# Scores on 64 instead of 32 partition rows, with the attention work moved to other places in the matmul stream, for batches 4 to 7

## The chip, the cores and the metric

One core of one Trainium2 chip. The metric is the device time of one execution in microseconds (us), as the median of several runs. The time before is 330.08 us. Runs of one kernel differ: those of the kernel before by up to 1.7% within the rounds of one chip (328.38 to 334.06). So every kernel is compared with runs of the kernel before on the same chip in the same rounds. Some runs are slow (more than 1.5% above the fastest of the same kernel). They take no part in any ratio, but are counted in the medians; of the profiles, only that of e3 is of a slow run.

## The reference

Two parts follow each other. The attention has 8 batches, 8 heads, 576 positions and 64 elements a head, and each head is computed twice: with a mask that leaves 7 neighbours, and on queries, keys and values that are averaged over 4 positions. The sum of both, as 4608 tokens of 512 features, goes through a feed-forward layer of 2048 features.

```python
def _attn_ref(q, k, v):                       # q, k, v: (8, 8, 576, 64) f32
    q_d = q.reshape(B, H, Sd, factor, D).mean(axis=3)      # factor 4; k_d, v_d too
    out_up = np.repeat(sm_attn(q_d, k_d, v_d), factor, axis=2)
    mask = np.abs(pos[:, None] - pos[None, :]) < factor
    scores = np.where(mask, scale * q @ k^T, -1e9)
    return out_up + softmax(scores) @ v
    # ... cut, written shorter
def _moe_ref(x, w_in, w_out):                 # (4608, 512), (512, 2048), (2048, 512)
    h = x @ w_in
    g = h * (1.0 / (1.0 + np.exp(-1.702 * h)))
    return (g @ w_out).astype(np.float32)
```

The inputs q and k are drawn with a factor of 0.1, which makes the softmax almost flat. So the check says little about the scores.

## The kernel before

The feed-forward layer runs in nine groups of 512 tokens. A group has 64 matmuls of the first product (16 slices of 4) and then 64 of the second, all 128x128 by 512 columns. Into this stream TensorE also gets the attention of the next batch, in seven pieces at fixed positions: position 0 to 15 is a slice of the first product, 16 and up counts the matmuls of the second.

```python
POS = [13, 16, 33, 42, 53, 62, 71]    # scores 0, exps 0, scores 1, values 0+1, values 2+3, transposes 0+1, 2+3

    for g in range(n_groups):
        b = g + 1
        # ... cut: group 0 has its own order
        elif b < B:
            if b > 2:
                load_v4(b)                       # SP: 6 DMAs, values to be averaged
            prep_qk(b, 0)                        # DVE: transposes k and q of heads 0 to 3 ("set 0")
            pool_qk(b, 0)                        # POOL: averages them
            if b + 1 < B:
                for qd in range(NQ):
                    load_qk(b + 1, qd)           # POOL: asks for the next batch's q and k
            prep_v(b, nc.gpsimd)                 # POOL: casts values to bf16
            if b + 1 < B:
                load_v(b + 1)                    # SP: 10 DMAs, next batch's values
            prep_qk(b, 1)                        # the same for heads 4 to 7 ("set 1")
            pool_qk(b, 1)
            prep_v4(b, nc.gpsimd)                # POOL: averages values
        # ... cut: the pieces of attention are put at POS; mm1, mm2
```

The DVE transposes take pairs of elements as one (the bitcast below). The kernel then reads a head of 64 elements from 32 partition rows, even and odd elements beside each other, and a score takes two matmuls of 32 rows (index `a`; 32*64 in the trace):

```python
    def prep_1(name, b, qd):
        # ... cut
        nc.vector.transpose(
            out=t32.rearrange("p (i c) -> p c i", c=18),
            in_=store[b, qd].bitcast(FP32).rearrange("p (c d) -> p c d", c=18),
        )

    def scores(b, qd, barred=False):             # 80 matmuls; scores_d: 24 in the same way
        # ... cut
        for i in range(5):
            for a in range(2):
                for par in range(2):
                    for r in range(4):
                        rows = slice(32 * r, 32 * r + 32)
                        # ... cut
                            lhsT=kT[b, qd][rows, k0 : k0 + 64, a],
                            rhs=qT[b, qd][rows, q0 : q0 + 60, a],
                            start=(a == 0 and not barred),
                            tile_position=(32 * r, 64 * par),
```

SP issues the value loads and the stores of the results, in program order. POOL issues the loads of q and k between its own sums.

The softmax here doesn't subtract the row's maximum and nothing guards it: scores larger than these inputs give would overflow.

## Time and profile before

330.08 us (329.90 to 331.29, 4 runs). The page of the kernel before, its span, engines, and two rows of its 40 slices (granted TensorE clock and DMA share in tenths):

```profile
span 329.5 us, 11220 instructions
PE 308.0 (93%) x4987; PEld 157.9 (48%) x5043; DVE 130.2 (40%) x215; ACT 184.1 (56%) x322; POOL 138.9 (42%) x168
PEclk9997999999999999999999999999999999999999
DMA  7999979999814991398339922993180110011011
```

TensorE (PE) is the bound (93% busy), at full clock (mean 0.995). The DMA row is not busy all the time: full for half a group, then nearly empty, and so on through groups 1 to 5.

Windows of the kernel before over groups 1, 3, 4 and 5. Columns: window and length, busy us (and instructions) of PE, PEld, DVE, ACT and POOL, then clock, DMA share and GB/s.

```profile
67.08:102.18 35.10, 33.30 (x594) 17.04 (x600) 17.43 (x27) 21.73 (x39) 17.52 (x19) 1.00 0.74 161
...
135.89:169.42 33.53, 32.63 (x594) 16.88 (x600) 16.33 (x25) 20.95 (x36) 17.53 (x19) 1.00 0.68 143
169.42:202.82 33.40, 32.50 (x595) 16.74 (x601) 16.34 (x25) 20.95 (x36) 17.51 (x19) 1.00 0.68 144
202.82:237.13 34.31, 32.79 (x594) 16.85 (x600) 16.33 (x25) 20.95 (x36) 17.51 (x19) 1.00 0.69 140
```

The 128 large matmuls of a group take 27.6 us (group 7, without attention). The rest of 33.4 us is attention, on the critical path because PE is nearly always busy.

PE's timeline of the kernel before at one score block (start, duration, what ran):

```profile
113.50 0.84 PE L351 MATMUL pa<-qT,kT 32*64 32x60 bf16 x80
114.14 0.59 PE L370 MATMUL pa<-qdT,kdT 32*64 32x144 bf16 x24
114.66 2.76 PE L618 MATMUL pm<-xT,w_in_bf 128*128 128x512 bf16 x11
```

From start to start, a block takes 114.66 - 113.50 = 1.16 us. That is what the change wants to halve.

SP's timeline of the kernel before in group 4 (start, us on its queue, what it issued):

```profile
170.67 2.95 SPq L226 DMA_DIRECT2D v<-in_v_dram  x6
179.43 8.90 SPq L214 DMA_DIRECT2D vf<-in_v_dram  x10
189.14 14.83 SPq L664 DMA_DIRECT2D out_dram<-osb  x4
```

An entry counts the waits inside it. The 14.83 us for four stores are almost all waiting for results; 0.33 us is one store. The value requests of 2.95 and 8.90 us are mostly issue time: over the whole run, one that loads values for the cast holds SP for a median of 0.64 us. In this kernel nothing that PE needs soon stands behind them.

### The profile page before, as it was taken

How to read it: one execution, taken by the hardware profiler on the slowest of the kernel's cores; microseconds unless marked ns; L12 is line 12 of the kernel's file. 1: busy time of each engine (PE TensorE's matmuls, PEld its weight loads, DVE VectorE, ACT ScalarE, POOL GpSimd, SP SyncE). 2: the span in 40 equal slices, each digit the busy share in tenths (PEclk: the TensorE clock that was granted, in tenths of full speed). 3: DMA queues.
4: the chain of work that ended last, by engine and by line, in shares of the span. 5: the costliest groups of instructions: out<-in, count | busy, mean ns of one | idle time of the engine just before them, and what ended most of it. 6: DMA issues, size and time to landing. Idle time of an engine off the chain costs nothing.

```text
span 329.5 us, 11220 instructions
## 1 busy us (share of the span) xinstructions
PE 308.0 (93%) x4987; PEld 157.9 (48%) x5043; DVE 130.2 (40%) x215; ACT 184.1 (56%) x322; POOL 138.9 (42%) x168
## 2 busy tenths in 40 slices
PE   8767999789999999999999999998999999999995
PEld 3444455445554455455544555455444544444444
DVE  4870512770468036802771277225730560000000
ACT  2552773375936683667367746674566646415611
POOL 7890844049603970298029901990098000000000
PEclk9997999999999999999999999999999999999999
DMA  7999979999814991398339922993180110011011
GB/s 126 184 188 208 171 151 183 196 210 236 191 39 132 205 207 39 116 193 171 102 100 200 200 83 86 196 195 105 40 172 2 60 41 32 2 72 56 2 62 65
DMA packets 63552, 41.36 MB, mean 126 GB/s; under 512 B 44048, under 2 KB 54416, under 8 KB 63504
## 3 DMA queue, kind: packets, MB, share of 16 engines
q1 hardware_dynamic: 55056, 26.95, 35.8%
q0 software_dynamic: 8304, 13.63, 23.9%
q8 instruction: 39, 0.64, 0.9%
q14 instruction: 9, 0.07, 0.1%
q10 hardware_dynamic: 144, 0.07, 0.1%
HBM read 44.83 MB, written 9.44 MB: 165 GB/s over the span
## 4 chain that ended last, share of the span: by engine, by line
PE 87%; issue 4%; SPq 3%; ACT 2%; DVE 2%; DMA 1%; DVEq 0%; ACTq 0%
PE pm L618 35%; PE pm L674 33%; PE pa L351 3%; SPq L214 3%; PE pa L618 2%; PE pa L431 2%; PE pa L409 2%; PE pa L370 2%; PE pa L458 2%; PE pa L674 2%; DMA vf<-in_v_dram 1%; PE pm L689 1%; PE pa L484 1%; ACT vd L321 0%; PE pa L312 0%
## 5 line engine op out<-in xcount | busy, mean ns | idle before, releaser
L618 PE MATMUL pm<-xT,w_in_bf 128*128 128x512 bf16 x528 | 120.3, 380 | 1.4 <-DVE xT L561 0.7
L674 PE MATMUL pm<-w_out_bf,gT 128*128 128x512 bf16 x493 | 114.1, 379 | 5.4 <-issue 5.2
L629 ACT ACTIVATE gT<-pm 128x512 bf16<-128x512 f32 x136 | 81.0, 598 | 45.2 <-PE pm L618 45.2
L618 PEld LDWEIGHTS <-w_in_bf 128*128 128x128 bf16 x576 | 55.8, 98 | 68.4 <-issue 2.5
L674 PEld LDWEIGHTS <-gT 128*128 128x128 bf16 x560 | 51.7, 98 | 59.5 <-issue 0.2
L276 POOL TENSOR_TENSOR pq<-kT 128x576 f32<-128x576 bf16 x16 | 18.5, 1157 | 105.0 <-DVE kT L260 96.1
L395 DVE TENSOR_TENSOR es<-es,mask 128x600 bf16<-128x600 bf16 x28 | 20.6, 749 | 92.0 <-ACT es L381 91.2
L659 ACT ACTIVATE osb<-pm 128x512 f32<-128x512 f32 (+2 forms) x35 | 20.7, 592 | 40.2 <-PE pm L674 36.1
L534 ACT COPY od<-pa 128x384 f32<-128x384 f32 (+1 forms) x56 | 18.4, 412 | 32.4 <-DVE y L444 18.7
L444 DVE TENSOR_TENSOR y<-pa,rc 128x896 bf16<-128x896 f32 x32 | 34.9, 1092 | 1.1
L555 DVE TENSOR_TENSOR xT<-pa,od 128x570 bf16<-128x570 f32 x28 | 21.1, 753 | 12.0 <-ACT od L534 11.9
L381 ACT ACTIVATE es<-pa 128x600 bf16<-128x600 f32 x32 | 19.8, 668 | 7.0 <-PE pa L351 6.8
L297 POOL TENSOR_TENSOR v<-v 112x512 f32<-112x512 f32 x18 | 22.8, 1265 | 0.0
L661 DVE TENSOR_SCALAR osb<-pm 128x128 f32<-128x128 f32 x1 | 0.3, 292 | 55.3 <-ACT osb L659 55.3
L260 DVE STREAM_TRANSPOSE kT<-kb 128x576 f32<-128x576 f32 x16 | 20.0, 1249 | 2.0 <-DMA kb<-in_k_dram 2.0
L260 DVE STREAM_TRANSPOSE qT<-qb 128x576 f32<-128x576 f32 x16 | 19.8, 1239 | 0.9 <-DMA qb<-in_q_dram 0.7
L276 POOL TENSOR_TENSOR pq<-qT 128x576 f32<-128x576 bf16 x16 | 18.4, 1148 | 0.0
L291 POOL CAST vb<-vf 128x2560 bf16<-128x2560 f32 (+1 forms) x11 | 17.6, 1618 | 0.0
L442 DVE RECIPROCAL rc<-pa 128x14 f32<-128x14 f32 x32 | 7.7, 240 | 21.7 <-PE pa L431 21.7
L351 PE MATMUL pa<-qT,kT 32*64 32x60 bf16 x1280 | 14.0, 203 | 1.5 <-issue 1.5
L351 PEld LDWEIGHTS <-kT 32*64 32x64 bf16 x1280 | 11.8, 104 | 6.7 <-issue 5.5
L300 POOL TENSOR_TENSOR vd<-v 112x256 bf16<-112x256 f32 x18 | 13.7, 759 | 1.4
(90 smaller groups left out, 247.0 us busy)
## 6 DMA issues: line engine op xcount, KB each, us to landing
vf<-in_v_dram SPq DMA_DIRECT2D x80, 128.0 KB, 4.7
out_dram<-osb SPq DMA_DIRECT2D x35, 256.0 KB, 2.1
v<-in_v_dram SPq DMA_DIRECT2D x36, 192.0 KB, 6.1
kb<-in_k_dram POOLq DMA_DIRECT2D x16, 288.0 KB, 6.8
qb<-in_q_dram POOLq DMA_DIRECT2D x16, 288.0 KB, 7.1
w_out_bf<-in_moe_w_out_dram POOLq DMA_DIRECT2D x4, 512.0 KB, 12.1
w_in_bf<-in_moe_w_in_dram POOLq DMA_DIRECT2D x2, 512.0 KB, 5.7
w_in_bf<-in_moe_w_in_dram POOLq DMA_DIRECT2D x1, 1024.0 KB, 10.7
```

What stands on the lines that cost most here:

```text
L260: nc.vector.transpose(out=t32.rearrange("p (i c) -> p c i", c=18), in_=store[b, qd].bitcast(FP32).rearrange("p (c d) -> p c d", c=18),)
L276: nc.gpsimd.tensor_tensor(out=t1, in0=sv[:, :, 0:2, :], in1=sv[:, :, 2:4, :], op=ALU.add)
L297: eng.tensor_tensor(out=t1[0:112], in0=x[:, :, 0:2, :], in1=x[:, :, 2:4, :], op=ALU.add)
L351: nc.tensor.matmul(sp[r // 2][64 * par : 64 * par + 64, r % 2, 60 * i : 60 * i + 60], lhsT=kT[b, qd][rows, k0 : k0 + 64, a], rhs=qT[b, qd] ...
L381: nc.scalar.activation(out=es[2 * qd + u][:, :, 0:300], in_=sp[u][:, :, 0:300], func=AF.Exp, scale=inv_sqrt_d,)
L395: nc.vector.tensor_tensor(out=ev, in0=ev, in1=mask, op=ALU.mult)
L444: nc.vector.tensor_tensor(out=y, in0=ov[:, :, :, 0:D], in1=rc.to_broadcast([128, 2, 7, D]), op=ALU.mult,)
L555: eng.tensor_tensor(out=sub(xT[hp], t0 + 3, (57, 2), (114, 5), (1, 57)), in0=sub(x, 3, (509, 2), (57, 5), (1, 57)), in1=sub(od, 3, (57, 2) ...
L618: nc.tensor.matmul(acc, lhsT=w_in_bf[:, dmc, ffc * 128 : (ffc + 1) * 128], rhs=xT[dmc][:, g * TG : g * TG + TG], start=(dmc == 0), stop=(d ...
L629: nc.scalar.activation(out=gT[:, ffc, :], in_=acc, func=AF.Silu, scale=GELU_SCALE)
L659: eng.activation(out=osb, in_=ap, func=AF.Copy, scale=1.0 / GELU_SCALE)
L674: nc.tensor.matmul(ops[t], lhsT=gT[:, ffc, t * 128 : (t + 1) * 128], rhs=w_out_bf[:, ffc, :], start=(ffc == 0), stop=(ffc == n_ffc - 1),)
```

## The change

The intent is to put a whole head of 64 elements on 64 rows, so that a score block needs 40 + 12 matmuls instead of 80 + 24. A second transpose of the same data and four SBUF-to-SBUF copies of 32 rows for each tile (k or q of one set) bring the odd elements beside the even ones. SP issues them, 64 in all. To give this chain time, the scores of batches 4 to 7 move one group earlier (a "rotated" pipeline), and loads, casts and sums are ordered anew. The diff, cut to its core:

```diff
+    ROWS64 = 4
 def prep_1(name, b, qd):
-        tt = work.tile([128, S, 2], BF16, ...)
-        nc.vector.transpose(...)
+        n = 2 if b >= ROWS64 else 1
+        tt = work.tile([128, 2, S, 2], BF16, ...)
+        for x in range(n):
+            # ... cut: the transpose, into tt[:, x]
+        if n == 2:
+            for x in range(2):
+                f = tt[:, x].rearrange("p t a -> p (t a)")
+                for r in range(2):
+                    src = 64 * r + 32 * x
+                    to = 64 * r + 32 * (1 - x)
+                    nc.sync.dma_start(
+                        out=f[to : to + 32, 0 : 2 * S - 1], in_=f[src : src + 32, 1 : 2 * S]
+                    )
 def scores(b, qd, barred=False):
+        if b >= ROWS64:                    # 40 matmuls, no accumulation
+            # ... cut: loops over j, i, par, u
+                            rows = slice(64 * u, 64 * u + 64)
+                                lhsT=kT[b, qd][rows, j, k0 : k0 + 64, 0],
+                                rhs=qT[b, qd][rows, j, q0 : q0 + 60, 0],
+                                start=True, stop=True,
+                                tile_position=(64 * u, 64 * par),
 # ... cut: scores_d and pool_qk in the same way; groups 0 and 2
-    POS = [13, 16, 33, 42, 53, 62, 71]
+    at(1, 0, load_qks, 3)                  # group 1, position 0, loads of q and k of batch 3
+    at(1, 0, prep_v, 2, nc.gpsimd)
+    at(1, 0, load_v, 3)
+    at(1, 0, prep_qk, 2, 1)
+    at(1, 0, load_qks, 4)                  # new in group 1
+    # ... cut
+    at(2, 68, s_all, 4, 0, False, True)    # scores of batch 4, set 0
+    at(3, 0, prep_v, 5, nc.gpsimd)
+    at(3, 0, prep_qk, 4, 1)                # copies of batch 4, set 1
+    # ... cut
+    at(3, 15, s_pe, 4, 1)
+    at(3, 52, s_all, 5, 0, False, False)
+    at(3, 64, s_all, 5, 1, False, True)
+    for g in range(4, B - 1):
+        b, c = g + 1, g + 2
+        if c < B:
+            at(g, 0, prep_v, c, nc.gpsimd)
+            at(g, 0, prep_qk, c, 0)        # copies of set 0
+            at(g, 0, pool_qk, c, 0)
+            at(g, 0, load_v4, c)
+            if c + 1 < B:
+                at(g, 0, load_v, c + 1)    # values, between the two sets of copies
+            at(g, 8, prep_qk, c, 1)        # copies of set 1
+            at(g, 8, pool_qk, c, 1)
+            if c + 1 < B:
+                at(g, 8, load_qks, c + 1)
+            at(g, 8, prep_v4, c, nc.gpsimd)
+            at(g, 42, s_all, c, 0, True, False)
+            at(g, 60, s_all, c, 1, False, True)
+        at(g, 6, avn, b, P01)              # values and transposes, now early
+        at(g, 11, avn, b, P23)
+        at(g, 16, tr, b, P01)
+        at(g, 25, tr, b, P23)
```

More of the change, by code (lines that the diff above doesn't have):

```diff
@@ L66 @@
     kdT = [persist.tile([128, 160, 2], BF16, name=f"kdT{i}") for i in range(NQ)]
+    kdP = [persist.tile([128, 2, 160], BF16, name=f"kdP{i}") for i in range(NQ)]
     PA = [psum.tile([128, 2, 512], FP32, name=f"pa{i}") for i in range(3)]
@@ L124, in fill @@
             nc.vector.memset(t[:, SD:160, :], 0.0)
+        for t in kdP:
+            nc.vector.memset(t[:, :, SD:160], 0.0)
         for t in vbs:
@@ L188, with load_1 @@
     qf, kf, vf = {}, {}, {}
-    def load_1(name, src, store, b, qd):
+    def load_1(name, src, store, b, qd, gate=None):
         t = ldp.tile(
@@ L193, in load_1 @@
         )
+        if gate is not None:
+            gate(t[0:1, 0:1])
         nc.gpsimd.dma_start(
@@ L201, in load_1, with load_qk @@
         store[b, qd] = t
-    def load_qk(b, qd):
-        load_1("k", k, kf, b, qd)
+    def load_qk(b, qd, gate=None):
+        load_1("k", k, kf, b, qd, gate)
         load_1("q", q, qf, b, qd)
@@ L257, in prep_1 @@
         store, dst = {"k": (kf, kT), "q": (qf, qT)}[name]
-        tt = work.tile([128, S, 2], BF16, name=f"{name}T{qd}", tag=f"{name}T{qd}", bufs=1)
-        t32 = tt.rearrange("p t a -> p (t a)").bitcast(FP32)
-        nc.vector.transpose(
-            out=t32.rearrange("p (i c) -> p c i", c=18),
-            in_=store[b, qd].bitcast(FP32).rearrange("p (c d) -> p c d", c=18),
-        )
-        dst[b, qd] = tt
+        n = 2 if b >= ROWS64 else 1
+        tt = work.tile([128, 2, S, 2], BF16, name=f"{name}T{qd}", tag=f"{name}T{qd}", bufs=1)
+        for x in range(n):
+            t32 = tt[:, x].rearrange("p t a -> p (t a)").bitcast(FP32)
+            nc.vector.transpose(
+                out=t32.rearrange("p (i c) -> p c i", c=18),
+                in_=store[b, qd].bitcast(FP32).rearrange("p (c d) -> p c d", c=18),
+            )
[7 more added lines that the diff above has]
+                        out=f[to : to + 32, 0 : 2 * S - 1], in_=f[src : src + 32, 1 : 2 * S]
+                    )
+        dst[b, qd] = tt if n == 2 else tt[:, 0]
     def prep_qk(b, qd):
@@ L273, in pool_qk @@
                 continue
+            if b >= ROWS64:
+                sv = src[b, qd].rearrange("p x (j f) a -> p (x j) f a", f=4)[:, :, :, 0]
+                t1 = work.tile([128, 2 * SD, 2], FP32, name="pq", tag="pq", bufs=1)
+                nc.gpsimd.tensor_tensor(
+                    out=t1, in0=sv[:, :, 0:2], in1=sv[:, :, 2:4], op=ALU.add
+                )
+                if name == "k":
+                    dst = kdP[qd][:, :, 0:SD]
+                else:
+                    dst = work.tile([128, 2, SD], BF16, name=f"qdT{qd}", tag=f"qdT{qd}", bufs=1)
+                    qdT[b, qd] = dst
+                t1 = t1.rearrange("p (x j) f -> p x j f", x=2)
+                nc.gpsimd.tensor_tensor(
+                    out=dst, in0=t1[:, :, :, 0], in1=t1[:, :, :, 1], op=ALU.add
+                )
+                continue
             sv = src[b, qd].rearrange("p (j f) a -> p j f a", f=4)
-            t1 = work.tile([128, SD, 2, 2], FP32, name="pq", tag="pq")
+            t1 = work.tile([128, SD, 2, 2], FP32, name="pq", tag="pq", bufs=1)
             nc.gpsimd.tensor_tensor(
@@ L341, in scores @@
         sp = [ps_tile(), ps_tile()]
+        if b >= ROWS64:
+            for j in range(2):
+                for i in range(5):
+                    for par in range(2):
+                        for u in range(2):
+                            rows = slice(64 * u, 64 * u + 64)
+                            k0 = 114 * i + KSTART[par]
+                            q0 = 114 * i + QSTART[par]
+                            nc.tensor.matmul(
+                                sp[u][64 * par : 64 * par + 64, j, 60 * i : 60 * i + 60],
+                                lhsT=kT[b, qd][rows, j, k0 : k0 + 64, 0],
+                                rhs=qT[b, qd][rows, j, q0 : q0 + 60, 0],
+                                start=True, stop=True,
+                                tile_position=(64 * u, 64 * par),
+                            )
+            return sp
         if barred:
@@ L363, in scores_d @@
         sd = sd or ps_tile()
+        if b >= ROWS64:
+            for kc in range(3):
+                for j in range(2):
+                    for u in range(2):
+                        rows = slice(64 * u, 64 * u + 64)
+                        nc.tensor.matmul(
+                            sd[64 * j : 64 * j + 64, u, SD * kc : SD * kc + SD],
+                            lhsT=kdP[qd][rows, j, 48 * kc : 48 * kc + 64],
+                            rhs=qdT[b, qd][rows, j, :],
+                            start=True, stop=True,
+                            tile_position=(64 * u, 64 * j),
+                        )
+            return sd
         bank = sd if sd is PM else [sd[:, u, :] for u in range(2)]
@@ L576, in warm, with s_pe, s_act, s_all @@
                 )
-    def attention(b, slots=None):
-        st = {}
-        def s_pe(qd):
-            st["s", qd] = scores(b, qd)
-            st["d", qd] = scores_d(b, qd)
-        def s_act(qd):
-            if qd == 0:
-                nc.scalar.preload_act_table_set("exp_and_others")
-            exp_local(qd, st["s", qd])
-            exp_down(qd, st["d", qd])
-            if qd == 1:
-                nc.scalar.preload_act_table_set("silu_and_others")
-            mask_local(qd)
-        def s1():
-            s_pe(1)
-            s_act(1)
-        def avn(*hps):
-            def f():
-                for n, hp in enumerate(hps):
-                    st["o", hp] = av(b, hp, slots and slots[n])
-                for hp in hps:
-                    st["y", hp] = normalise(st["o", hp])
-            return f
-        def tr(*hps):
-            def f():
-                for n, hp in enumerate(hps):
-                    st["x", hp] = transp(st["y", hp], slots and slots[n])
-                for hp in hps:
-                    od = copy_od(st["x", hp])
-                    merge(b, hp, st["x", hp], od)
-            return f
-        return [lambda: s_pe(0), lambda: s_act(0), s1, avn(0, 1), avn(2, 3), tr(0, 1), tr(2, 3)]
+    st = {}
+    def s_pe(b, qd):
+        st["s", b, qd] = scores(b, qd)
+        st["d", b, qd] = scores_d(b, qd)
+    def s_act(b, qd, first, last):
+        if first:
+            nc.scalar.preload_act_table_set("exp_and_others")
+        exp_local(qd, st["s", b, qd])
+        exp_down(qd, st["d", b, qd])
+        if last:
+            nc.scalar.preload_act_table_set("silu_and_others")
+    def s_all(b, qd, first, last):
+        s_pe(b, qd)
+        s_act(b, qd, first, last)
+        mask_local(qd)
+    def avn(b, hps, slots=None):
+        for n, hp in enumerate(hps):
+            st["o", hp] = av(b, hp, slots and slots[n])
+        for hp in hps:
+            st["y", hp] = normalise(st["o", hp])
+    def tr(b, hps, slots=None):
+        for n, hp in enumerate(hps):
+            st["x", hp] = transp(st["y", hp], slots and slots[n])
+        for hp in hps:
+            od = copy_od(st["x", hp])
+            merge(b, hp, st["x", hp], od)
     def hps_mm(g, ffc, dmc, acc):
@@ L701, in mm2 @@
             f()
-    POS = [13, 16, 33, 42, 53, 62, 71]
-    POS_0 = [16, 18, 27, 54, 68, 60, 76]
-    VDP_0 = 52
     o, y, x = {}, {}, {}
@@ L800, with at, load_qks @@
         silu(gT0, ffc, acc[ffc])
-    def loads_2():
-        load_v(2)
-        load_v4(2)
+    P01, P23 = (0, 1), (2, 3)
+    plans = {g: {} for g in range(n_groups)}
+    def at(g, pos, f, *args):
+        plans[g].setdefault(pos, []).append(lambda: f(*args))
+    def load_qks(b):
+        for qd in range(NQ):
+            load_qk(b, qd)
+    at(0, 16, s_pe, 1, 0)
+    at(0, 18, s_act, 1, 0, True, False)
+    at(0, 18, mask_local, 0)
+    at(0, 27, s_all, 1, 1, False, True)
+    at(0, 52, prep_vd_pe, 1, PA[2])
@@ new lines @@
+    at(0, 54, avn, 1, P01, (1, 2))
+    at(0, 60, tr, 1, P01, (1, 2))
+    at(0, 68, avn, 1, P23, (1, 2))
+    at(0, 76, tr, 1, P23, (1, 2))
+    at(1, 0, prep_qk, 2, 0)
+    at(1, 0, pool_qk, 2, 0)
+    at(1, 0, load_qks, 3)
[3 more added lines that the diff above has]
+    at(1, 0, load_qks, 4)
+    at(1, 0, pool_qk, 2, 1)
+    at(1, 0, prep_v4, 2, nc.gpsimd)
+    at(1, 13, s_pe, 2, 0)
+    at(1, 16, s_act, 2, 0, True, False)
+    at(1, 16, mask_local, 0)
@@ new lines @@
+    at(1, 33, s_all, 2, 1, False, True)
+    at(1, 42, avn, 2, P01)
+    at(1, 53, avn, 2, P23)
+    at(1, 62, tr, 2, P01)
+    at(1, 71, tr, 2, P23)
+    at(2, 0, load_v4, 3)
+    at(2, 0, prep_qk, 3, 0)
+    at(2, 0, pool_qk, 3, 0)
+    at(2, 0, prep_qk, 3, 1)
+    at(2, 0, load_qks, 5)
+    at(2, 0, prep_v, 3, nc.gpsimd)
+    at(2, 0, pool_qk, 3, 1)
+    at(2, 0, prep_v4, 3, nc.gpsimd)
+    at(2, 13, s_pe, 3, 0)
+    at(2, 13, prep_qk, 4, 0)
+    at(2, 13, pool_qk, 4, 0)
+    at(2, 13, load_v, 4)
@@ new lines @@
+    at(2, 16, s_act, 3, 0, True, False)
+    at(2, 16, mask_local, 0)
+    at(2, 29, s_all, 3, 1, False, False)
+    at(2, 38, avn, 3, P01)
+    at(2, 47, avn, 3, P23)
+    at(2, 49, load_v4, 4)
+    at(2, 49, prep_v, 4, nc.gpsimd)
+    at(2, 49, prep_v4, 4, nc.gpsimd)
+    at(2, 54, tr, 3, P01)
+    at(2, 61, tr, 3, P23)
+    at(2, 66, load_v, 5)
+    at(2, 68, s_all, 4, 0, False, True)
+    at(3, 0, prep_v, 5, nc.gpsimd)
+    at(3, 0, prep_qk, 4, 1)
+    at(3, 0, pool_qk, 4, 1)
+    at(3, 0, load_v4, 5)
@@ new lines @@
+    at(3, 6, avn, 4, P01)
+    at(3, 7, prep_qk, 5, 0)
+    at(3, 7, pool_qk, 5, 0)
+    at(3, 15, s_pe, 4, 1)
+    at(3, 15, prep_qk, 5, 1)
+    at(3, 15, pool_qk, 5, 1)
+    at(3, 15, load_qks, 6)
+    at(3, 15, prep_v4, 5, nc.gpsimd)
+    at(3, 15, load_v, 6)
+    at(3, 16, s_act, 4, 1, True, False)
+    at(3, 16, mask_local, 1)
+    at(3, 26, tr, 4, P01)
+    at(3, 34, avn, 4, P23)
+    at(3, 43, tr, 4, P23)
+    at(3, 52, s_all, 5, 0, False, False)
+    at(3, 64, s_all, 5, 1, False, True)
@@ L806 @@
     for g in range(n_groups):
-        b = g + 1
         if g == 0:
@@ L820 @@
                 prep_v(1, nc.gpsimd, i=slice(i, i + 1))
-            for qd in range(NQ):
-                load_qk(2, qd)
-            loads_2()
-        elif b < B:
-            if b > 2:
-                load_v4(b)
-            prep_qk(b, 0)
-            pool_qk(b, 0)
-            if b + 1 < B:
-                for qd in range(NQ):
-                    load_qk(b + 1, qd)
-            prep_v(b, nc.gpsimd)
-            if b + 1 < B:
-                load_v(b + 1)
-            prep_qk(b, 1)
-            pool_qk(b, 1)
-            prep_v4(b, nc.gpsimd)
-        steps = {}
-        if b < B:
-            for n, f in zip(POS if g else POS_0, attention(b, None if g else (1, 2))):
-                steps.setdefault(n, []).append(f)
-            if g == 0:
-                steps.setdefault(VDP_0, []).append(lambda: prep_vd_pe(1, PA[2]))
+            load_qks(2)
+            load_v(2)
+            load_v4(2)
+        steps = plans[g]
         gT = new_gT() if g else gT0
```

## The prediction

> **What bounds it.** TensorE. The page gives PE 93% busy (ACT 56, POOL 42, DVE 40); the chain of waits is 87% PE; the clock is full. No PE wait in groups 2 to 6 lasts over 0.7 us. In PE's timeline these groups last 33.4 to 34.3 us, of which 128 512-column matmuls at 0.216 us (48 in 10.4 us) are 27.6; a batch's attention is so about 6 us, all on the critical path. Groups 7 and 8 have none.
>
> **Removed.** For batches 4 to 7 each score block loses half its instructions: 80 pairs (weight load and matmul) of 32 rows become 40 of 64, and 24 become 12 (program order: 832 PE rows fewer). Timeline: the 80 take 0.64 us, 8 ns a pair; the 24 take 0.52 us, 22 ns each. Are 64-row pairs slower? The existing 64x64 value matmuls (65 columns) run 20 in 0.18 us, 9 ns, so the rate goes by pairs, not rows. [...] Estimate: 40 x 9 ns + 12 x 22 ns = 0.62 us for 1.17, 0.54 us saved, eight blocks: 4.3 us.
>
> **Added.** 16 DVE transposes (1.09 us apart, 17 us in all), 64 SBUF-to-SBUF copies of 32 rows on SP, 2 memsets. POOL's sums keep their size. Off the critical path except where an in-order queue makes PE wait.
>
> **Moved.** From batch 4 on scores run one group earlier. The crossing, groups 2 and 3, is tight:
> - Scores of (3,1) come four matmuls (0.86 us) earlier, while exps hold the PSUM tiles (before: tile free at 221.25, scores at 221.66): about 0.4 us.
> - Scores of (4,0) come 7 matmuls after batch 3's last transposes; merging took 3.06 us from their start, 2.7 are left: 0.4 us. Its exps (2.2) and table load (1.28) exceed the 2.6 us left of the group: 0.4 us.
> - Values: one load takes about 11 us (first issue 112.2, DMA quiet at 123.5) and its buffer is single. Batch 5's starts only when 4's are cast, at about 30 us of group 2, and the copies of (4,1) stand behind it on SP. Pooled q of (4,1) is ready at about 14.7 us of group 3, PE wants it at 14.5. Each us later is a us of PE wait.
> - In group 3 DVE transposes (5,1) before it masks (4,1) and merges: second value block 0.9, second transposes 0.7 us.
> About 3 us lost, estimated. In groups 4 to 6 I find about a us of slack.
>
> **Net.** 330.1 - 4.3 + 3, less some of the 0.6 us issue gap of group 5: 328.3 us, range 325.3 to 331.3. Faster by over 2%: 0.05; within 2%: 0.91; slower: 0.04.
>
> **To check.** Score blocks of the new shape: 40 in about 0.36 and 12 in about 0.26 us. Groups 2 and 3 hold three score blocks, 35 to 36 us each; 4 and 5 about 32.6; 6, without scores, about 31. Group 3's PE waits name pooled q/k, masks or merges. DVE busy about 150 us, POOL as before.
>
> **What would make it wrong.** 64-row pairs paced by rows: no gain. Copies that land late behind value loads: waits of several us in groups 3 to 5, even a lower clock. Instruction fetch starving ("issue" gaps; one of 2.9 us at 23.5 us, when DMA is full), as value blocks now stand where DMA is busiest. If the author's positions fit the chip better than my sums, 325.5.

The sum stays 330.1 - 4.3 + 3, less some 0.5: 328.3 us.

## The result, and the profile after

The changed kernel takes 344.81 us (344.12 to 345.39, 4 runs) against 330.08: a ratio of 1.0437, 95% interval 1.0406 to 1.0469. It is slower.

The page of the kernel after:

```profile
span 343.5 us, 10647 instructions
PE 317.7 (92%) x4627; PEld 156.5 (46%) x4627; DVE 148.5 (43%) x233; ACT 181.8 (53%) x320; POOL 141.7 (41%) x168
PEclk9998999999999999996999998799999999999999
DMA  7999789899937957969389595966110020011012
```

There are 360 fewer PE records (the program has 416 matmuls fewer; some records are missing), yet PE is busy longer, 317.7 us for 308.0. The clock row shows why: slices with 6 and 7 tenths that were full before. The quiet stretches of the DMA row are mostly filled up to the middle of the span.

Windows of the kernel after over groups 1, 3, 4 and 5, columns as before:

```profile
66.80:104.21 37.41, 34.25 (x601) 17.00 (x600) 17.93 (x27) 21.72 (x39) 20.40 (x23) 1.00 0.85 189
...
140.09:179.70 39.61, 37.01 (x549) 17.54 (x548) 25.32 (x34) 23.11 (x40) 23.47 (x26) 0.91 0.76 162
179.70:221.03 41.33, 35.02 (x497) 16.76 (x496) 21.77 (x31) 21.05 (x36) 19.29 (x22) 0.92 0.88 179
221.03:253.68 32.65, 32.65 (x497) 15.98 (x496) 17.61 (x27) 20.94 (x36) 17.53 (x17) 1.00 0.46 116
```

| group | before, us | after, us | difference |
|---|---|---|---|
| 1 | 35.10 | 37.41 | +2.3 |
| 2 | 33.71 | 35.88 | +2.2 (it has three score blocks) |
| 3 | 33.53 | 39.61 | +6.1 (it has three score blocks) |
| 4 | 33.40 | 41.33 | +7.9 |
| 5 | 34.31 | 32.65 | -1.7 |
| 6 | 33.40 | 30.80 | -2.6 (it has no scores) |

With 0.3 us gained before group 1 and nothing changed after group 6, this is the 14.0 us between the profiled spans. Group 5 is as I predicted (32.6) and has no wait over 0.2 us. The loss is in groups 1, 3 and 4.

PE's timeline of the kernel after at group 4. The bracket is the idle time before the entry and what ended it.

```profile
172.13 0.52 PE L383 MATMUL pa<-qT,kT 64*64 64x60 bf16 x40
172.53 0.38 PE L418 MATMUL pa<-qdT,kdP 64*64 64x144 bf16 x12
172.85 2.76 PE L729 MATMUL pm<-w_out_bf,gT 128*128 128x512 bf16 x12
...
210.61 0.18 PE L383 MATMUL pa<-qT,kT 64*64 64x60 bf16 x1 [3.47 <-DMA qT<-qT]
...
212.42 0.48 PE L383 MATMUL pa<-qT,kT 64*64 64x60 bf16 x19 [0.46 <-DMA qT<-qT]
214.68 0.57 PE L418 MATMUL pa<-qdT,kdP 64*64 64x144 bf16 x12 [1.78 <-POOL qdT L303]
215.19 6.01 PE L729 MATMUL pm<-w_out_bf,gT 128*128 128x512 bf16 x20
```

Three readings. The new score block is short: 172.85 - 172.13 = 0.72 us. The second set of copies of batch 6 is late by 3.47 us, the copies after it 0.43, 0.17 and 0.46 more (two of these lines are left out), and its pooled q, summed from the copies' rows, adds 1.78: 6.31 us in all. Then 20 large matmuls take 6.01 us where, at the 0.216 us that one takes in group 7 of the kernel before (64 in 13.81 us from start to start), 20 would take 4.3 us. The clock of that stretch is 0.59 (215.2 to 219.0 us).

SP's timeline of the kernel after over the same group tells why the copies are late:

```profile
170.92 10.47 SPq L220 DMA_DIRECT2D vf<-in_v_dram  x10
181.49 4.18 SPq L719 DMA_DIRECT2D out_dram<-osb  x4
185.77 2.99 SPq L278 DMA_DIRECT2D kT<-kT  x4
188.87 2.73 SPq L278 DMA_DIRECT2D qT<-qT  x4
191.70 4.21 SPq L232 DMA_DIRECT2D v<-in_v_dram  x6
196.00 9.77 SPq L220 DMA_DIRECT2D vf<-in_v_dram  x10
205.88 2.47 SPq L278 DMA_DIRECT2D kT<-kT  x4
208.44 2.43 SPq L278 DMA_DIRECT2D qT<-qT  x4
```

SP has hardly a pause: from 185 to 212 us the waits that its view names sum to 2.9 us. Where it once waited 14.83 us for stores, the stores of group 3 stand in its queue behind values, and PE asks for the copies at about 207.1 us (210.61 - 3.47) when the last four have not been issued. A copy of 72 KB holds SP for a median of 0.54 (q) to 0.58 us (k), and lands in a median of 2.1 (q) to 2.9 us (k) from its issue. The entries of the sixty-four add up to 41.0 us of SP's time.

PE's timeline of the kernel after in group 1, at values of batch 2:

```profile
90.83 0.23 PE L493 MATMUL pa<-vd,ed 48*64 48x65 bf16 x5 [0.47 <-POOL vd L333]
92.83 0.23 PE L493 MATMUL pa<-vd,ed 48*64 48x65 bf16 x5 [1.78 <-issue]
```

This 0.47 + 1.78 us is nearly the whole loss of group 1 (2.3 us), which has no new kind of work, only the request for q and k of batch 4. In the second, "issue" means that the profile shows no other engine to have held PE back. Windows there, of the kernel before and of the kernel after:

```profile
88.00:92.00 4.00, 3.68 (x114) 2.17 (x108) 2.17 (x5) 3.27 (x4) 0.03 (x1) 1.00 0.59 156
```
```profile
88.00:92.00 4.00, 2.58 (x42) 1.14 (x42) 1.84 (x2) 2.85 (x4) 2.70 (x3) 1.00 1.01 203
```

The DMA share is 1.01 instead of 0.59 (it adds up the packets' times, so it can pass 1). Two theories were taken to the experiments. **Theory A**: SP's serial issue makes the copies late. **Theory D**: when the DMA engines are full, PE's own instruction fetch, which also goes over DMA (the page lists an instruction queue), starves. The rivals were the 64-row shape itself, the copies' load on the DMA engines, and the new positions of the pieces.

The instruction queue on the page of the kernel before (packets, MB, share of the 16 engines' span):

```profile
q8 instruction: 39, 0.64, 0.9%
```

The records of these packets, of 16 KB each, bear on theory D. In the packed traces of all 14 kernels TensorE has 67 idle times of over 0.5 us that end in "issue". Every one of them ends 1.21 to 1.65 us after such a packet has landed. The 78 waits of that length for which another cause is named end anywhere from 0.14 to 24 us after one. And in each of the 49 "issue" gaps of over 0.9 us, the mean DMA share of the 2 us before that packet started was 0.94 or more.

### The profile page after: what moved, and what is told of

It is laid out like the page before. It is cut to its first block, busy times and chain, and to the rows that moved or that the text cites. A ratio compares the mean times of both kernels' runs of the same rounds, so it can differ in the third digit from the quotient of the medians.

```text
span 343.5 us, 10647 instructions
## 1 busy us (share of the span) xinstructions
PE 317.7 (92%) x4627; PEld 156.5 (46%) x4627; DVE 148.5 (43%) x233; ACT 181.8 (53%) x320; POOL 141.7 (41%) x168
## 4 chain that ended last, share of the span: by engine, by line
PE 68%; SPq 9%; POOL 6%; DMA 6%; DVE 4%; issue 4%; ACT 2%; POOLq 0%; DVEq 0%; ACTq 0%
PE pm L729 27%; PE pm L673 27%; SPq L220 8%; DMA qT<-qT 2%; PE pa L673 2%; DMA vf<-in_v_dram 2%; PE pa L493 2%; DMA out_dram<-osb 2%; PE pa L729 2%; SPq L278 1%; DVE kT L268 1%; PE pa L471 1%; PE pa L520 1%; POOL v L330 1%; PE pm L744 1%
## 5 line engine op out<-in xcount | busy, mean ns | idle before, releaser
L673 PE MATMUL pm<-xT,w_in_bf 128*128 128x512 bf16 x544 | 123.5, 382 | 0.7 <-DVE xT L623 0.7
L729 PE MATMUL pm<-w_out_bf,gT 128*128 128x512 bf16 x528 | 123.8, 387 | 0.0
L729 PEld LDWEIGHTS <-gT 128*128 128x128 bf16 x560 | 52.9, 99 | 63.3 <-issue 5.1
L268 DVE STREAM_TRANSPOSE kT<-kb 128x576 f32<-128x576 f32 x24 | 28.6, 1246 | 16.4 <-POOL kdT L318 7.3
L506 DVE TENSOR_TENSOR y<-pa,rc 128x896 bf16<-128x896 f32 x32 | 34.9, 1092 | 1.1
L268 DVE STREAM_TRANSPOSE qT<-qb 128x576 f32<-128x576 f32 x24 | 28.5, 1238 | 1.1 <-DMA qb<-in_q_dram 1.1
L617 DVE TENSOR_TENSOR xT<-pa,od 128x570 bf16<-128x570 f32 x28 | 21.1, 754 | 15.8 <-ACT od L596 15.6
L330 POOL TENSOR_TENSOR v<-v 112x512 f32<-112x512 f32 x18 | 24.2, 1345 | 0.9 <-DMA v<-in_v_dram 0.9
L324 POOL CAST vb<-vf 128x2560 bf16<-128x2560 f32 (+1 forms) x11 | 17.4, 1603 | 16.9 <-DMA out_dram<-osb 11.0
L493 PE MATMUL pa<-vd,ed 48*64 48x65 bf16 x640 | 12.3, 194 | 3.1 <-issue 2.1
L449 ACT ACTIVATE ed<-pa 128x864 bf16<-128x864 f32 x15 | 13.4, 896 | 1.1 <-PE pa L418 1.1
```

Of the source, the lines that this page charges most:

```text
L268: nc.vector.transpose(out=t32.rearrange("p (i c) -> p c i", c=18), in_=store[b, qd].bitcast(FP32).rearrange("p (c d) -> p c d", c=18),)
L330: eng.tensor_tensor(out=t1[0:112], in0=x[:, :, 0:2, :], in1=x[:, :, 2:4, :], op=ALU.add)
L493: nc.tensor.matmul(o[64 * pos : 64 * pos + 64, j, c0 : c0 + 65], lhsT=Ed[64 * j : 64 * j + 48, u, q0 : q0 + 64], rhs=vd[64 * j : 64 * j + ...
L506: nc.vector.tensor_tensor(out=y, in0=ov[:, :, :, 0:D], in1=rc.to_broadcast([128, 2, 7, D]), op=ALU.mult,)
L617: eng.tensor_tensor(out=sub(xT[hp], t0 + 3, (57, 2), (114, 5), (1, 57)), in0=sub(x, 3, (509, 2), (57, 5), (1, 57)), in1=sub(od, 3, (57, 2) ...
L673: nc.tensor.matmul(acc, lhsT=w_in_bf[:, dmc, ffc * 128 : (ffc + 1) * 128], rhs=xT[dmc][:, g * TG : g * TG + TG], start=(dmc == 0), stop=(d ...
```

## The experiments

All twelve kernels gave a result marked correct. The table sums them up; "before" is the median of the same rounds.

| kernel | us | before, us | ratio [95%] |
|---|---|---|---|
| e1, no copies | 335.85 | 330.57 | 1.0146 [1.0072, 1.0220] |
| e2, new order with 32-row heads | 337.99 | 330.57 | 1.0185 [1.0089, 1.0280] |
| e3, values behind copies | 337.60 | 330.57 | 1.0174 [1.0088, 1.0259] |
| e4, 64 rows in the old order | 399.90 | 330.57 | 1.2088 [1.2011, 1.2166] |
| e5, e3 and batch 4's q, k asked for in group 2 | 338.26 | 330.48 | 1.0191 [1.0108, 1.0274] |
| e6, e5 and another order for group 3 | 340.17 | 330.48 | 1.0290 [1.0223, 1.0356] |
| e7, old positions, copies first | 335.90 | 330.48 | 1.0117 [1.0054, 1.0181] |
| e8, e7 from batch 2 on | 338.75 | 330.48 | 1.0149 [1.0067, 1.0232] |
| e9, e5 with the request held back | 334.29 | 331.36 | 1.0106 [1.0043, 1.0170] |
| e10, e7 with later scores | 350.84 | 331.36 | 1.0584 [1.0525, 1.0643] |
| e11, the kernel before with q, k asked for later | 345.43 | 331.36 | 1.0437 [1.0364, 1.0510] |
| e12, e10 with another order on POOL | 335.77 | 331.18 | 1.0126 [1.0076, 1.0177] |

### e1: no copies (wrong scores on purpose)

```diff
-                    nc.sync.dma_start(out=f[to : to + 32, 0 : 2 * S - 1], in_=f[src : src + 32, 1 : 2 * S])
+                    pass
```

> The 64 odd-element copies are left out, all else as in the changed kernel (the result is wrong on purpose: half of the rows hold the wrong elements). Theory A (SP's issue time: each copy holds SP's in-order queue for 0.58 us, 64 of them 38 us, and value loads of 10 us stand between them, so the second copies of a batch are issued after PE wants their scores): the waits on copies and pooled q/k in groups 3 and 4 go, with the half clock that follows them; groups 3 and 4 fall from 39.6 and 41.3 to about 34.5 and 32.7 us, the whole to 327 to 330 us (group 1 keeps its 2.3 us). Theory B (the rotated order itself, DVE's doubled transposes and POOL behind them): the copies matter little, 338 us or more, the waits renamed to DVE and POOL.

The odd elements are then wrong, but every matmul, transpose and sum stays. Group 4 falls from 41.3 to 34.5 us and group 3 from 39.6 to 35.0; the waits for copies and for pooled q are gone. About 9 us of the 14.7 so hang on the copies (ratio 1.0146 against 1.0437). The remaining 5 us do not: groups 1 and 2 are 39.0 and 36.5 us, not shorter than in the kernel after. With 335.85 us the run missed the ranges of both theories (327 to 330, 338 or more): A has the larger part, but not all. Group 4 stays over the expected 32.7 us, as a new "issue" gap of 1.78 us opens in it (at 192.11 us, DMA share 1.17).

### e2: the new order alone

```diff
-    ROWS64 = 4
+    ROWS64 = 99
```

> The rotated schedule with 32-row scores for all batches: no second transposes, no copies, a correct result. Theory A: rotation alone costs little; 80+24 pairs in place of 40+12 cost 0.45 us more in each of eight blocks, so about 3.6 us over the run without copies, 330.5 to 334 us. Theory B: the rotated order makes the waits, 338 us or more.

337.99 us. With 32-row heads, without one copy or second transpose, the new order alone costs 1.9%. Groups 1 to 3 are 38.1, 36.4 and 38.5 us. So a loss remains even without the 64-row path, and at 338 us this is theory B's outcome (338 or more), and not theory A's (330.5 to 334). It lies 2.1 us above e1 by the medians, not 3.6, and their intervals overlap, so these two runs do not show what the 64-row shape saves over the whole kernel. It has "issue" gaps of 1.8 us in group 1 and 1.7 us in group 3; in the second, at 169 to 171 us, the DMA share is 1.07.

### e3: values behind the copies

```diff
-                at(g, 0, load_v, c + 1)
             at(g, 8, prep_qk, c, 1)
             at(g, 8, pool_qk, c, 1)
+            if c + 1 < B:
+                at(g, 8, load_v, c + 1)
```

> In groups 4 and 5 the values of the next batch are requested after the second set of copies, not between the sets; group 3 is left. Theory A: the copies of (6,1) are issued about 10 us earlier and group 4 falls from 41.3 to 32.7 to 33.5 us; group 3 stays near 39.6; the whole 335 to 337.5 us. Rival C ([...] a copy lands late wherever it is issued): the copies land over 5 us after issue and group 4 stays over 37 us.

337.60 us; the profiled run, 340.28, is the slow one, so take its lines for the order of things more than for the time. SP's timeline of e3 in group 4:

```profile
196.45 3.02 SPq L232 DMA_DIRECT2D v<-in_v_dram  x6
199.57 2.42 SPq L278 DMA_DIRECT2D kT<-kT  x4
202.09 3.58 SPq L278 DMA_DIRECT2D qT<-qT  x4
205.75 7.15 SPq L220 DMA_DIRECT2D vf<-in_v_dram  x10
```

PE's timeline of e3, at the same score block:

```profile
209.67 0.52 PE L383 MATMUL pa<-qT,kT 64*64 64x60 bf16 x40
211.35 0.38 PE L418 MATMUL pa<-qdT,kdP 64*64 64x144 bf16 x12 [1.16 <-POOL qdT L303]
```

Nothing is removed, only the place in SP's queue. The wait for copies is gone, that for the pooled q falls from 1.78 to 1.16 us, and group 4 takes 33.7 us for 41.3. The load on the DMA engines is the same, so for group 4 it is the order in SP's queue, as theory A has it, and not the rival of the copies' bytes, that makes most of the loss. Rival C is seen in part: two k copies land 5.9 and 6.3 us after their issue. Groups 1 and 3 (38.0, 38.9) stay, as the edit does not touch them.

### e4: 64 rows in the old order

```diff
-    # the rotated plan
+    # the kernel before's order of loads and POS = [13, 16, 33, 42, 53, 62, 71], with ROWS64 = 4
```

> 64-row scores from batch 4 on in the schedule of the kernel before (values requested between the two sets, scores at positions 13 and 33 of the same group). Theory A: the copies then have less time still; scores (b,0) wait about 3 us and scores (b,1) about 8 us in each of groups 3 to 6, with the half clock after, so 365 to 385 us. Theory B (rotation is what costs): faster than the changed kernel, under 340 us.

399.90 us. The largest of PE's waits in e4 (who waited for whom: us in total, times, longest):

```profile
PE pa L383 <- DMA qT<-qT: 26.1, 14, 8.1
```

The pooled q adds 16.4 us. Groups 3 to 5 take 54.2 to 54.8 us, far more than I had thought. In the old order the copies of set 1 stand behind ten value requests, and the scores are due in the same group. Issue time is not all of it. In group 3 SP stands 8.7 us for POOL's cast of the values that hold the buffer (`SPq L220 <- POOL vb L324: 8.7, 1, 8.7`), and this cast stands in POOL's queue behind the sums of set 0. The author's rotation is an answer to this. The e7 below does the same work in another order of queueing, so the 54 us are the queues' and not the work's.

### e5: the request for batch 4's q and k one group later

```diff
-    at(1, 0, load_qks, 4)
+    at(2, 0, load_qks, 4)      # first of group 2; and e3's edit
```

> On top of e3: batch 4's q and k are requested at the start of group 2 and not in group 1. Theory D (the rotated order puts attention's many short instructions where DMA is full, and PE's own instruction fetch then starves): group 1 loses the issue gap of about 1.8 us in its first value block and the wait of 0.5 us for the downsampled values, and falls from 38.0 to about 35.1 us, at most 35.6; the DMA share just before that block falls from over 1.0 to about 0.6; the whole is about 2.5 us under e3, 334 to 336 us. If that gap has nothing to do with these loads, group 1 stays at 37 to 39 us.

338.26 us: it missed the expectation of a shorter group 1, which became 40.7 us instead. In the trace of e5 POOL ran ahead of PE, and issued the first of these loads at 88.25 us, still in group 1. That made a cleaner test than the one I had planned. PE's timeline of the kernel before, then of e5, at the same ten matmuls of group 1 (the nine before them start at 94.34 and 94.28 us):

```profile
94.80 0.29 PE L431 MATMUL pa<-vd,ed 48*64 48x65 bf16 x10 [0.19 <-issue]
```
```profile
97.95 0.38 PE L493 MATMUL pa<-vd,ed 48*64 48x65 bf16 x10 [3.40 <-issue]
```

Windows of the kernel before, then of e5, over that time:

```profile
94.50:98.00 3.50, 2.99 (x84) 1.71 (x74) 2.55 (x4) 0.43 (x2) 0.00 (x0) 1.00 0.19 66
```
```profile
94.50:98.00 3.50, 0.10 (x11) 0.04 (x7) 1.25 (x2) 0.00 (x0) 0.00 (x0) 0.80 1.01 231
98.00:102.00 4.00, 3.67 (x18) 1.38 (x18) 1.34 (x2) 0.00 (x0) 0.00 (x0) 0.50 0.10 23
```

Up to here PE has the same matmuls in the same order in both kernels, and no tile is named as missing. With the DMA share at 0.19, the ten matmuls start after 0.19 us; at 1.01, after 3.40 us. After the gap the clock is at 0.50, and group 1 is 5.6 us longer than in the kernel before, more than the gap. In the DMA records, a packet of 16 KB on the instruction queue starts at 91.92 us in the kernel before and has landed at 93.35; the ten matmuls start 1.45 us later. In e5 it starts at 95.71 us and has landed at 96.65, and the ten matmuls start 1.30 us later. Theory D fits this, and no other engine or tile is in the way.

### e9: e5 with the request really held back

```diff
-    at(2, 0, load_qks, 4)
+    # the k tile is first written by a one-element DVE copy that waits for group 2's first transpose
+    at(2, 0, load_qk, 4, 0, gate=after(kT[3, 0][0:1, 0, 0:1], nc.vector))
```

> e5 with the request for batch 4's q and k held back by a one-element copy on DVE behind the first transpose of group 2: in e5 POOL ran ahead of the program's groups and issued it at 88.3 us, inside group 1, just ahead of the value blocks (DMA share 1.01 at 94.5 to 98 us, against 0.19 before) and the same ten matmuls that waited 0.19 us for issue before waited 3.40. Theory D (instruction fetch starves when DMA is full): in group 1 the DMA share around the second value block falls under 0.3, the gap to under 0.3 us, group 1 to 34.8 to 35.3 us. Otherwise the gap stays over 1 us although DMA is quiet.

The edit is shown shortened. Now the loads are issued at 106.3 us. Window of e9:

```profile
94.50:98.00 3.50, 3.34 (x92) 1.72 (x91) 2.71 (x5) 0.36 (x1) 0.00 (x0) 1.00 0.22 80
```

The gap is gone and group 1 takes 34.8 us for e5's 40.7, with the DMA share back at 0.22. So the load in group 1 made the gap. The median falls only to 334.29 us, since the gate delays POOL and group 2 has a new wait of 1.93 us for averaged values, with half the clock after it (eight large matmuls take 3.49 us, for 1.89 elsewhere), so that group 2 takes 39.2 us. A gain in one group was partly given back in the next.

### e6: another order for group 3

```diff
+    at(2, 62, prep_qk, 4, 1)
+    at(2, 62, pool_qk, 4, 1)
-    at(3, 0, prep_v, 5, nc.gpsimd)
-    at(3, 0, prep_qk, 4, 1)
-    at(3, 0, pool_qk, 4, 1)
-    at(3, 7, pool_qk, 5, 0)
+    at(3, 15, prep_v, 5, nc.gpsimd)
+    at(3, 15, pool_qk, 5, 0)      # both after load_qks(6); on top of e5
```

> On top of e5: the second transposes and copies of batch 4 come at the end of group 2, ahead of batch 5's values, and POOL sums them before it casts these values. Theory A (SP's order and issue time): the waits for copies and pooled q/k in group 3 (about 2.5 us) and the half clock behind them (2 to 3 us) go; group 3 falls from 38.9 to 34.5 to 35.5 us, the whole to 329 to 332 us. If the waits come from the length of the value loads alone, group 3 stays over 37 us.

340.17 us. The wait for the copies of batch 4, set 1, is gone as expected, but it turned up again at batch 5, set 0 (1.94 + 0.46 us for copies and 1.81 for pooled q), and group 3 takes 43.3 us. My expectation of a gain fell. In e6's SP queue the values (7.61 us from 144.65 us), a store with its wait (4.08) and the averaged values' loads (4.42) stand ahead of the copies of batch 5: moving one item forward made the others late. The edit also moves a cast and sums on POOL, so the 1.81 us need not be SP's alone.

### e7 and e8: old positions, copies first in the queue

```diff
-    # the rotated plan
+    # POS of the kernel before but scores 0 at 15; for b >= ROWS64 each group queues:
+    # prep_qk(b, 0), prep_qk(b, 1), prep_v, prep_v4, pool_qk(b, 0), load_qks/load_v/load_v4 of b + 1, pool_qk(b, 1)
```

e8 is e7 with `ROWS64 = 2`.

> 64-row scores from batch 4 on, not rotated, but SP gets a batch's 16 copies first in its group, then the next values; values are cast first, first scores at position 15 in place of 13. Theory A: 16 copies take about 9.5 us of SP from 2.3 us of the group on, so the first scores (about 13 us) and the second (about 20 us) find their data: groups 3 to 6 take 32.5 to 33 us in place of 33.4 to 34.3, against 54 us in e4 with the same work in another order; the whole 326 to 328.5 us, up to 1.2% under the kernel before. Theory B (64 rows with copies cannot pay at all because copies crowd the DMA): groups 3 to 6 over 33.5 us, 331 us or more.

> e7 from batch 2 on (groups 1 to 6). Theory A: two more groups gain 0.9 us each: 324 to 327.5 us, the best of all. Theory D limits it: groups 1 and 2 carry more DMA, so an issue gap of 1 to 2 us may take the gain back, then about 328 us.

e7 takes 335.90 us, and its groups 3 and 5 take 33.5 and 33.8 us where e4 took 54.8 and 54.7. This is the same work with the same copies, in another order on the queues (SP's and POOL's, and the first scores two slices later), and confirms what e4 meant. But group 4 takes 36.5 us, and it is no gain on the kernel before: three waits for pooled q, 4.2 us in all, are left. I had expected 326 to 328.5 us; the outcome is the one that I had written down for theory B (331 us or more), and the trace gives it a cause: before each of these sums POOL itself waits 2.8 to 3.8 us for a q copy of set 1. Most copies land 2.0 to 2.1 us after their issue, but in groups 3, 4 and 5 one of these q copies lands after 4.4, 6.3 and 6.5 us, while the loads of q, k and values that are requested just behind it fill the DMA engines (share 1.10 at 186 to 192 us). So once SP's order is mended, the DMA load may be the next limit, and the rival that copies and loads crowd each other is not out. e8, with 96 copies, has five such waits (5.8 us), one of 1.5 us for a copy, and four "issue" gaps of 0.53 to 1.28 us from group 1 on, for one of 1.49 in e7; by their intervals it can't be told from e7, so doing it for more batches gained nothing (324 to 327.5 us expected).

### e10 and e12: later scores

```diff
+    # e7 with score blocks at 24 and 40, values at 47 and 55, first transposes at 63
+    # e10: pool_qk(b, 0) ahead of prep_v4;  e12: prep_v, prep_v4, requests, then pool_qk(b, 0), pool_qk(b, 1)
```

> e7 with the score blocks at positions 24 and 40 in place of 15 and 33 from batch 4 on, POOL's sums of the first set ahead of the downsampled values, and batch 4's downsampled values requested in group 3, not 2. Theory A: the waits of 1.0 to 1.8 us for pooled q in groups 3 to 5 and the half clock after them go; these groups take 32.5 us; group 2 is back at 33.7 us; the whole 326.5 to 330 us, 0 to 1% under the kernel before. If issue gaps appear in the value blocks (DMA is fuller than before by 16 copies), 330 to 333 us.

> e10 failed by an order of mine: POOL stood with the second set's sums behind the downsampled values and the requests, so PE waited 2.4 to 7.2 us for pooled q. Here POOL casts the values, sums the downsampled values (loaded a group earlier), requests q and k about 9 us into the group, then sums both sets as their copies land (ready at about 15 and 19 us; PE wants them at 15.5 and 20.3). Theory A and D: no wait for copies or pooled q over 0.5 us except in group 3, where the downsampled values are requested ahead of the copies; groups 4 and 5 take 32.5 to 33.5 us, the whole 328 to 333 us. Issue gaps of 1 to 2 us in value or transpose blocks remain possible, as the next downsampled values are still in flight there; with more than two of them it is no better than the kernel before.

e10 failed, and through a mistake of mine in POOL's order: PE waited four times for pooled q, 13.8 us in all and up to 7.2.

e12 mends the order: one such wait of 3.1 us is left, in group 3, and one "issue" gap of 2.3 us in group 4. Group 5 takes 33.4 us, as expected (32.5 to 33.5), group 4 with its gap 34.9. At 335.77 us it missed the 328 to 333 and is not distinguishable from e7. No version that I tried beats the kernel before.

### e11: the kernel before with one request moved

```diff
             pool_qk(b, 0)
-            if b + 1 < B:
-                for qd in range(NQ):
-                    load_qk(b + 1, qd)
             prep_v(b, nc.gpsimd)
             # ... cut
             prep_v4(b, nc.gpsimd)
+            if b + 1 < B:
+                for qd in range(NQ):
+                    load_qk(b + 1, qd)
```

> The kernel before with one thing moved: in groups 1 to 5 POOL requests the next batch's q and k after its last sum of the group (about 20 us into the group) and not after its first (about 6 us). PE's program is the same to the instruction, nothing waits for these loads until the next group, 13 us later. Theory D: the loads now run beside the value and transpose blocks; issue gaps of 1 to 3.5 us appear in each of groups 1 to 5 and some half clock after them: 336 to 346 us. If issue gaps do not depend on DMA load: within 2 us of the kernel before.

This is the direct test of theory D: no 64-row heads, no copies, no rotation, the same PE program, the same bytes. In POOL's timeline of group 5 the request starts at 233.57 us, 17.6 us into the group, instead of 208.30, 5.5 us into it. So its data come when the attention's many small matmuls run. The time rises to 345.43 us. Waits of e11:

```profile
PE pa L431 <- issue: 11.9, 5, 3.6
```

PE's timeline of e11 at the longest:

```profile
242.44 0.49 PE L431 MATMUL pa<-vd,ed 48*64 48x65 bf16 x17 [3.56 <-issue]
243.26 2.92 PE L674 MATMUL pm<-w_out_bf,gT 128*128 128x512 bf16 x7 [0.33 <-issue]
```

Five gaps, one in each of groups 1 to 5, are 11.9 us of the 17.6 by which the profiled run (348.94 us, the slowest of four fast ones) is over the median before. The one of group 3 has only 0.77 us, where I had expected 1 or more; after the longest, 7 large matmuls take 2.92 us instead of 1.5, which is the half clock again (mean 0.64 from 242.5 to 247.0 us). The instruction packet here runs from 240.08 to 240.96 us, and PE goes on 1.48 us after it, much as in e5. So where the DMA engines are full is worth 4% of this kernel by itself. That this load is off the critical path by every wait in the profile did not protect PE. (That the ratio equals the changed kernel's is chance; the causes are not the same.)

## Why the prediction was wrong, point by point

I predicted 328.3 us (325.3 to 331.3) and "within 2%" with 0.91. It is 344.81.

- **The saving: right mechanism, a little too large.** I wrote "40 x 9 ns + 12 x 22 ns = 0.62 us for 1.17, 0.54 us saved, eight blocks: 4.3 us." Measured: 40 in 0.40 us and 12 in 0.32, so 0.72 a block, 0.45 us saved, 3.6 us. In the trace a 64-row pair costs little more than a 32-row one (10 ns for 8). Groups 5 and 6 came out as predicted (32.65 and 30.80 us). The rival "64-row pairs paced by rows" is out.
- **The crossing of group 2: right.** Waits of 0.27 and 0.40 us, for 0.4 and 0.4 predicted; 35.88 us for "35 to 36". A third 0.4 us, for exps and table load at the group's end, is not in the trace. Of group 3 I had named value blocks and transposes as late by 0.9 and 0.7 us; neither wait is in the trace, which has other ones there.
- **The failed step: "In groups 4 to 6 I find about a us of slack."** Behind it stands the sum for SP's queue: I counted the 64 copies as work "Off the critical path except where an in-order queue makes PE wait", and gave them no duration. The mechanism was named, even "Each us later is a us of PE wait" for group 3, and "Copies that land late behind value loads" stood among the risks, but with 0.04 for "slower": the term was mis-sized. A copy holds SP for 0.54 to 0.58 us, 16 of them in group 4 stand there for 10.6 us with their waits (2.99 + 2.73 + 2.47 + 2.43), beside 9.77 for values, 4.21 for the averaged values' loads and 4.18 for delayed stores. In group 4 that was no slack but 6.31 us of waits, in group 3 another 2.54. From the trace of before I could have formed it: a value request holds SP for a median of 0.64 us there and a store for 0.33, so 64 DMAs would be some 41 or 21 us, an estimate; 41.0 were measured.
- **The clock after waits: named, not counted.** "even a lower clock" stood among the risks. In group 4, 20 matmuls took 6.01 us for 4.3; in group 3, 14 took 5.77 (158.31 to 164.08 us) for 3.02. That is 1.7 + 2.75, some 4.4 us. Window of the kernel after in group 3, clock 0.54 (in group 4 it is 0.59):

```profile
158.30:164.10 5.80, 5.80 (x22) 1.92 (x18) 3.19 (x5) 3.85 (x5) 0.11 (x1) 0.54 0.94 186
```

- **The DMA's quiet time: named as a risk, given no us.** "Instruction fetch starving ("issue" gaps...)". It cost 2.3 us in group 1 of the kernel after, through a load moved there. My text gave group 1 no line, although the change adds a load there. The runs showed that a load also has to stay out of the way of PE's fetch: e5 against e9 for this load (a gap of 3.40 us, and none), e11 for the kernel before (11.9 us in five gaps).

Adding up for the kernel after, as an estimate: waits 6.31 + 2.54, clock 4.4 and the gap of group 1 with 2.3 are 15.6 us, and the smaller saving is 0.7. Less the 2.0 us of waits that I had counted and that did not come (1.6 in group 3, 0.4 in group 2), this is 14.3 of the 16.5 us by which the prediction missed (344.8 - 328.3). Some 2 us are not assigned.

What stays open: why the new order alone (e2) costs 1.9% to the last us, as its gaps of 1.8 and 1.7 us and the clock are only part of it; and whether a version with fewer copies, which SP could issue in time and which landed in time, would gain the 3.6 us. That the "issue" gaps are waits for instruction packets is inferred from the 1.21 to 1.65 us in all 67 cases, and e5, e9 and e11 show that moving a load makes or removes them. Why a packet comes late when the DMA share is high is inferred; no run shows the queue inside the DMA engines. Nor did a run separate the clock's loss from the waits before it.

## What to carry to other kernels

Give each DMA a duration on the queue of the engine that issues it (here 0.54 to 0.58 us a copy on SP), and sum that queue for a stage, before calling added DMAs free: the consumer waits for the last item ahead of its own (3.47 us in group 4 of the kernel after), and then, as in e7, for a landing that took up to 6.5 us in place of 2 beside other loads. Look at when the DMA engines are idle as well as at how busy they are: a quiet stretch may be what lets a stage of many small matmuls run, and a load moved into it can cost TensorE more than the moved work saves (11.9 us of gaps in e11). In these runs an idle time of two or three us on TensorE could bring the half clock after it, and its length alone did not tell when: a gap of 1.80 us in e2's group 1 did (clock 0.62 from 91.0 to 95.5 us, where ten large matmuls took 4.01 us), one of 2.31 us in e12 did not (1.00 from 202.4 to 206.0, where eight took 1.90). In group 3 of the kernel after, waits of 0.18, 0.51 and 1.85 us within 3.1 us were followed by the 0.54.
